# A gated mix of linear attention and an MLP on one core: first tiles reordered, two loads and two pieces of work moved up, denominators stored beside their product

## The chip, the cores and the metric

The kernel runs on one core of a Trainium2 chip. The metric is the device time of one execution in microseconds (us), lower is better. The kernel before takes 1105.97 us (median of 3 runs, 1105.97 to 1106.19).

The engines are called as the profile does: PE (matrix products), PEld (its weight loads), DVE (vector), ACT (activations), POOL (a second, slower vector engine) and SP (here it only starts DMAs). Each engine runs its instructions in program order and waits for others by semaphores. DMAs are started from SP's queue, a few from ACT's.

## The reference

```python
def _A_ref(x, wqkv, wo):
    qkv = (x @ wqkv).reshape(B, S, 3, H, Dh).transpose(2, 0, 3, 1, 4)
    q, k, v = qkv[0], qkv[1], qkv[2]
    phi = lambda t: jnp.where(t > 0, t + 1, jnp.exp(t)) + 1e-6
    pq, pk = phi(q), phi(k)
    kv = jnp.einsum("bhsd,bhse->bhde", pk, v)
    z = jnp.einsum("bhsd->bhd", pk)
    num = jnp.einsum("bhqd,bhde->bhqe", pq, kv)
    den = jnp.einsum("bhqd,bhd->bhq", pq, z)[..., None] + 1e-6
    return (num / den).transpose(0, 2, 1, 3).reshape(B, S, D) @ wo

def _B_ref(x, w1, b1, w2, b2):
    y = _layernorm(x, axis=-1)
    h = gelu_tanh(y @ w1 + b1)
    return h @ w2 + b2

g = sigmoid((x * gate_w).sum(-1, keepdims=True))
return g * a + (1 - g) * b        # a from _A_ref, b from _B_ref
```

S = 2048 rows, D = 576 columns, 32 heads of 18 columns, and an inner width F = 4608 of the MLP; everything is float32.

## The kernel before

All products run at float32 accuracy on operands that are split into a high part (rounded by ACT's copy) and a low part (the rest, by a DVE subtraction). So almost every operand costs one ACT and one DVE instruction ahead of PE, and both must be done before PE can use it. All 576 rows of a contraction are five blocks of 128, the last one holding 64 rows twice ("tail": `xe`, `we`, loaded by `load_twice`, L137), so that its high and low parts share a block. The profile gives L113 as the line of nearly every instruction, because they all pass through the class `InOrder` (L113), which keeps each engine in the order of the program text. So instructions are told apart by tiles.

**First tiles** (L481 to L577). After WARM passes of a product of ones, three x tiles of 128 rows are loaded together with the key and query weights, in four halves (KEY 0, KEY 1, QUERY 0, QUERY 1). The tile `t` holds a raw x tile, `s` raw weights, `y` the splits of both. The gate's weights (`gw`, landing in a corner of `accs`) are loaded by two DMAs on ACT's queue, turned by five small transposes and put beside the second half of the key weights.

**Sweep** (the loop behind `for n in range(FIRST, NT)`). One x tile after another: keys (project, then phi on ACT and DVE into `k`, then the split `ks`), the sums over keys times x, and queries into `accs` or `acc_right`. Preparations for later run beside it: a table `jobs` holds for each third of a tile what is issued there (`at(n, ...)`: n is three times the tile's position plus 0, 1 or 2). Among them are the first two chunks of w1 (`sum_w1`, `early_part`, stored by `store_early` to `w1d` through the stages `ys`), the normalised x pairs (`normal_pair`, `sum_pair`, `split_pair`, stored to `yd`), and the load of the value weights `wv` (`load_wv` at place 38). Every such load and store goes to SP's one queue, between the x tiles that are loaded two positions ahead.

**Attention loop** (`for i in range(NT)`). For each tile: POOL multiplies the queries with the sum of keys (`weigh`, tile `qz`, three buffers, four tiles ahead), DVE reduces the product to 32 denominators (`normalize`: reduction, addition, reciprocal) and normalises the queries, PE transposes them, ACT and DVE split the transposes (`qt`), and PE multiplies with `wp`. Sums for later pairs run on POOL beside it in `w_raw` and `accs`.

**MLP** (windows w = 0 to 17, and a tail). The first product is done with seven products of sums of blocks in place of eight (Strassen and Winograd), over 18 chunks of w1, first for one half of the rows and then for the other; the second product runs a window later (tiles `h`, `w_ops`). Sums of blocks of h (`sum_h`) and of w2 run on POOL or DVE by a written table of places (`do`, `do_first`: window, step 0 to 14, job). In window 10 the first half is finished: `add_combined` adds the MLP's part to the attention's part (tile `w_raw` or `pks`) and `store_out` sends it off, one tile a step.

Of the kernel before, what the change touches and what calls it, by code (L numbers as in the profile page):

```python
# [9 lines left out]
F32 = mybir.dt.float32  # L10
# [7 lines left out]
P = 128  # L18
# [18 lines left out]
EARLY = 2  # L37
EPS_PHI = 1e-6
EPS_LN = 1e-5
WARM = 6  # L40
FIRST = 3
LATE = 3
X_RING = 4
# [53 lines left out]
def heads(ap):  # L97
    return ap.rearrange("p (h d) -> p h d", d=DH)
# [18 lines left out]
def tile_gated_mix(ctx: ExitStack, tc: tile.TileContext, x, xm, xe, wm, we, wvm, wve, wo, um, ue, w2, b1, b2, gw, out):  # L117
# [17 lines left out]
        return ps[:, next(ff_banks)]  # L135

    def load_twice(dst, src, by=sp):  # L137
        for half in range(2):
            by.dma_start(dst[half * 64:(half + 1) * 64], src)

    def four_times(ap, half):

# [75 lines left out]
    def load_w(part, half, pieces=((0, 5),), by=sp):  # L218
        if (part, half) not in wraw:
            wraw[part, half] = wsp.tile([P, 5, HALF + 2], F32, name="s", tag="s")  # L220
        s = wraw[part, half]
        main = wm[part * 2 + half].rearrange("p (t n) -> p t n", t=4)
        tail = we[part * 2 + half]
        for t0, t1 in pieces:
            if t0 < 4:
                by.dma_start(s[:, t0:min(t1, 4), :HALF], main[:, t0:min(t1, 4)])
            if t1 == 5:
                load_twice(s[:, 4, :HALF], tail, by)
# [8 lines left out]
    def load_x(i):  # L237
        xraw[i] = yt.tile([P, 5, P], F32, name="t")
        sp.dma_start(xraw[i][:, 0:4], xm[i].rearrange("p (t n) -> p t n", t=4))
        load_twice(xraw[i][:, 4], xe[i])  # L240

    def split_x(i, pieces=((0, 5),)):
        if i not in xs:
            xs[i] = x_places[PLACE[i] % X_RING]
        to, src = xs[i], xraw[i]
        for t0, t1 in pieces:
            act.activation(to[:, t0:t1], src[:, t0:t1], AF.Copy)
            if t0 < 4:
                dve.tensor_sub(to[:, 5:9], src[:, 0:4], raw(to[:, 0:4]))
            if t1 == 5:  # L250
                dve.tensor_sub(to[64:P, 4], src[64:P, 4], raw(to[64:P, 4]))
# [16 lines left out]
    def project(i, part, half, order=BY_ROWS, n=None):  # L268
        w = W[part, half]
        p = banks[i, part, half] = ps[:, next(halves_in) if n is None else n]  # L270
        for m, (a, b) in enumerate(order):
            pe.matmul(p[:, :w.shape[2]], xs[i][:, a, :], w[:, b], start=(m == 0), stop=(m == len(order) - 1))
# [208 lines left out]
    first = ORDER[:FIRST]  # L481
    gwr = spare[0:1, :5 * P]
    load_x(first[0])
    load_w(KEY, 0, ((0, 1), (1, 2), (2, 4)), act)
    act.dma_start(gwr[:, :D], gw.rearrange("(a n) -> a n", a=1))
    act.dma_start(gwr[:, D:], gw[4 * P:D].rearrange("(a n) -> a n", a=1))
    act.activation(tiny, ones[:, 0:1], AF.Exp)
    load_w(KEY, 0, ((4, 5),))
    load_x(first[1])
    load_w(KEY, 1)  # L490
    load_x(first[2])
    load_w(QUERY, 0)
    load_xn(first[0])
    load_w(QUERY, 1)
# [12 lines left out]
    def first_keys(n, half):  # L507
        project(first[n], KEY, half, HI_FIRST, 3 * half + n)

    def first_queries(n, half):  # L510
        project(first[n], QUERY, half, HI_FIRST)

    def both_phi(n):
        for half in range(2):
            keys_phi(first[n], half)


    column = ps[:, 7, :5]
    for t in range(5):
        pe.transpose(column[:, t:t + 1], gwr[:, t * P:(t + 1) * P], ident[0:1, 0:1])  # L520
    first_keys(0, 0)
    split_x(first[1])
    first_keys(1, 0)
    dve.tensor_copy(wraw[KEY, 1][:, :, HALF:HALF + 1], column[:, :, None])
    dve.memset(wraw[KEY, 1][:, :, HALF + 1:HALF + 2], 1.0)
    split_w(KEY, 1)
    split_x(first[2])
    load_x(ORDER[3])
    first_keys(0, 1)
    first_keys(1, 1)  # L530
    both_phi(0)
    split_w(QUERY, 0)
    first_keys(2, 0)
    first_keys(2, 1)
    both_phi(1)
    keys_split(first[0])
    first_queries(0, 0)
    first_queries(1, 0)
    both_phi(2)
    phi(acc[first[0]], first[0], QUERY, 0)  # L540
    split_xn(first[0])
    moments_of(first[0])
    load_xn(first[2])
    first_queries(2, 0)
    phi(acc[first[1]], first[1], QUERY, 0)
    for part in range(2):
        add_products(first[0], part)
    split_w(QUERY, 1)
    phi(acc[first[2]], first[2], QUERY, 0)
    first_queries(0, 1)  # L550
    first_queries(1, 1)
    keys_split(first[1])
# [30 lines left out]
    def at(n, f, *args):  # L583
        jobs[n].append(lambda: f(*args))
# [8 lines left out]

    at(3 * 5, sp.dma_start, b1s, b1)
    at(31, load_wo)
    at(38, load_wv)
    for n, f in ((24, gates_in), (25, gates_act), (26, gates_out)):
        at(n, f, 0)
    def prepare_scale(q, n):
# [2 lines left out]
        at(n + 2, share_moments, q)  # L602

    for k in range(EARLY):
        n0 = (10, 13)[k]
        for n in range(4):
            at(n0 + n // 2, sum_w1, k, n, dve)
            at(n0 + 1 + n, early_part, k, n)
            at(n0 + 2 + n, store_early, k, n)
# [76 lines left out]
    qz, qt, tails, abank = {}, {}, {}, {}  # L686

    def weigh(i):
        qz[i] = qzp.tile([P, D], F32, name="qz")
        pool.tensor_tensor(out=qz[i], in0=acc[i], in1=zb, op=OP.mult)  # L690

    dens = {}

    def normalize(i, parts=(0, 1)):
        if 0 in parts:
            dens[i] = small.tile([P, H], F32, name="den")
        den = dens[i]
        if 0 in parts:
            dve.tensor_reduce(out=den, in_=heads(qz[i]), op=OP.add, axis=AX.X)
            dve.tensor_tensor(out=den, in0=den, in1=den0, op=OP.add)  # L700
            dve.reciprocal(den, den)
        if 1 in parts:
            dve.scalar_tensor_tensor(heads(acc[i]), heads(acc[i]), EPS_PHI, den[:, :, None].to_broadcast([P, H, DH]),
                                     op0=OP.add, op1=OP.mult)
# [102 lines left out]
        sp.dma_start(late_acc[i], acc[i])  # L807


    def w1_places(k, first):  # L810
        a, b = FIRST_W if first else LAST_W
        return wa if first else wb, wr(k)[:, a:b + 1]

    def split_w1(k, first):
        w, src = w1_places(k, first)
        act.activation(w[:, :, 0:3], src, AF.Copy)

    def split_w1_rest(k, first):
        w, src = w1_places(k, first)
        dve.tensor_sub(w[:, :, 3:5], src[:, :, 0:2], raw(w[:, :, 0:2]))  # L820
        dve.tensor_sub(w[64:P, :, 2], src[64:P, :, 2], raw(w[64:P, :, 2]))

# [253 lines left out]
    for p in range(WINDOWS - 1):  # L1076
        w = p + 1
        if p == 0:
            for x, m in zip((12, 13, 14, 15), (T3, T1, T2, T4)):
                do(0, x, sum_w2, 0, m, dve)  # L1080
        for m in range(7):
            x = 2 * m - 2 * (p == m == 0)
            do_first(w, x + -2.0, prepare_hi, p, m)
            do_first(w, x + -1.5, prepare_h_lo, p, m)
            do_first(w, x + -1.5, prepare_w2_lo, p, m)
        for x, *a in ((0, S3), (3.3, S2), (6, S1, dve), (7, S4)) if p < HALF_PAIRS else ((0, S3), (3, S2), (6, S1), (7, S4)):
            do(w, x, sum_h, p, *a)
        for x, m in ((4, S3), (8, S2), (9, S1), (11, S4)):
            do(w, x, give_back, p, m)
        if p + 1 < HALF_PAIRS:  # L1090
            for x, m in ((1, B11), (1, B21), (3, B12), (4, B22)):
                do(w, x, load_w2, p + 1, (m,))
        else:
            do(w, 5, load_w2, p + 1)
        if p + 1 < WINDOWS - 1:
            for x, *a in ((8, T3, dve), (9, T1), (10, T2, dve), (12, T4)) if p + 1 < HALF_PAIRS else ((9, T3), (10, T1), (11, T2), (12, T4)):
                do(w, x, sum_w2, p + 1, *a)

    for k in range(HALF_TIME):
        w, x = k // 2, 7 * (k % 2)  # L1100
        if k >= EARLY:
            x1 = x + (0, 0)[k % 2] if k + 1 < HALF_TIME else x - 1
            do_first(w, x1 + 0.5, split_w1, k, False)
            do(w, x1, split_w1_rest, k, False)
            if k + 1 < HALF_TIME:
                do(w, x1, load_w1, k + 1, False)
            do(w, x1, store_w1, k, True)
            do(w, x1 + 1, store_w1, k, False)
        if EARLY <= k + 1 < HALF_TIME:
            for x1, n in zip((-1, 0, 1, 2) if k < EARLY else ((0, 1, 2, 3), (0, 1, 2, 4))[k % 2], (0, 1, 3, 2)):  # L1110
                do(w, x + x1, sum_w1, k + 1, n, dve)
            x1 = x + (4 if k < EARLY else (4, 4)[k % 2])
            do_first(w, x1 + 0.5, split_w1, k + 1, True)
            do(w, x1, split_w1_rest, k + 1, True)
            if k + 2 < HALF_TIME:
                do(w, x1, load_w1, k + 2, True)

# [3 lines left out]
    for s in range(TPS):  # L1121
        if s < 6:
            do(p + 1, 6 + s, load_late, s, s)
        else:
            do(p + 2, 4, load_late, s, s - 6)
        do(p + 2, 1 + s, add_combined, p, s, s % 6)
        do(p + 2, 1 + s, store_out, s, s % 6)

    h_stage = h_ops.rearrange("p c k a n -> p (c k a n)")
    h_stages = [stage_of(h_stage[:, n * 10 * P:(n + 1) * 10 * P]) for n in range(3)]  # L1130
# [122 lines left out]
```

## Time and profile before

| what | value |
|---|---|
| median of the runs | 1105.97 us |
| profiled execution | 1106.91 us, its span 1105.2 us |
| DVE busy | 881.5 us |
| ACT busy | 571.1 us |
| POOL busy | 308.1 us |
| moved by DMA | 206.21 MB |
| start-up and first tiles | 0 to 40 us of the span |
| sweep over the other tiles | 40 to 186 us |
| moments, attention loop | 186 to 282 us |
| MLP windows from the second on | 306.8 us to the end |

A row of a timeline reads: start, duration, engine, line, operation, out<-in, shape, count, and in brackets how long the engine had been idle before it, and which engine's or transfer's end released it. Rows of windows give, for each engine, the busy time with the number of instructions in brackets; then the granted clock of PE, the DMA share and the rate.

### The profile page before, as it was taken

The numbers are of one execution on the slowest core, as the hardware profiler recorded it, in microseconds if no ns is written. First come the engines' busy times: TensorE is split into PE (matmuls) and PEld (weight loads), VectorE is DVE, ScalarE is ACT, GpSimd is POOL, SyncE is SP. The second block draws the span as 40 slices with busy tenths as digits, with TensorE's granted clock in tenths as the row PEclk, the third lists the DMA queues.
The fourth block names the chain that finished last, engine by engine and source line by source line (L and its number), as shares of the span: only waits on it lengthen the run. The fifth ranks groups of instructions, "written<-read, shape, count | busy, mean of one in ns | idle before, by whom it ended". The sixth has DMA issues, their size and how long they took to land.

```text
span 1105.2 us, 17967 instructions
## 1 busy us (share of the span) xinstructions
PE 1088.0 (98%) x6651; PEld 995.6 (90%) x6651; DVE 881.5 (80%) x1292; ACT 571.1 (52%) x917; POOL 308.1 (28%) x218
## 2 busy tenths in 40 slices
PE   8999998999999999999999999999999999999998
PEld 8989997999879989889898899989999999999998
DVE  4699987799788999999999996895666656656687
ACT  5667665344566555555556454355444444444450
POOL 0000000871022232222312223342543424334400
PEclk9999999999999999999999999999999999999999
DMA  6475766676964645536445498655544434434342
GB/s 176 139 260 185 244 212 233 217 293 235 341 206 156 201 165 197 187 138 241 165 163 192 144 342 353 204 155 198 150 112 134 141 106 145 144 108 142 105 153 86
DMA packets 126972, 206.21 MB, mean 187 GB/s; under 512 B 9743, under 2 KB 82735, under 8 KB 122918
## 3 DMA queue, kind: packets, MB, share of 16 engines
q1 hardware_dynamic: 126322, 204.49, 55.4%
q8 instruction: 52, 0.85, 0.3%
q10 hardware_dynamic: 564, 0.59, 0.2%
q14 instruction: 34, 0.28, 0.1%
HBM read 135.95 MB, written 69.09 MB: 186 GB/s over the span
## 4 chain that ended last, share of the span: by engine, by line
PE 80%; DVE 12%; DMA 3%; issue 2%; ACT 2%; SPq 1%; ACTq 0%; DVEq 0%
PE ps L113 80%; DVE h L113 2%; DVE accs L113 2%; DVE wa L113 2%; DVE w_ops L113 1%; SPq L113 1%; ACT wa L113 1%; DVE u L113 1%; DMA t<-in_xe 1%; DVE w_raw L113 1%; DVE den L113 1%; DMA w1d<-ys 0%; DMA w2r<-in_w 0%; DVE w2r L113 0%; DVE acc_right L113 0%
## 5 line engine op out<-in xcount | busy, mean ns | idle before, releaser
L113 PEld LDWEIGHTS ps<-w_ops,h 128*128 128x128 f32 x2856 | 427.1, 188 | 42.6 <-DVE w_ops L113 4.4
L113 PE MATMUL ps<-w_ops,h 128*128 128x288 f32 x2856 | 452.7, 295 | 2.4 <-DVE w_ops L113 1.8
L113 PE MATMUL ps<-y,wa 128*128 128x512 f32 x1008 | 277.2, 393 | 1.6 <-DVE wa L113 1.2
L113 POOL TENSOR_TENSOR u<-u 128x512 f32<-128x512 f32 x118 | 179.5, 1547 | 282.3 <-DVE h L113 148.8
L113 DVE TENSOR_TENSOR accs<-ps,accs 128x576 f32<-128x576 f32 x210 | 158.2, 754 | 107.3 <-PE ps L113 100.3
L113 PE MATMUL ps<-y,wb 128*128 128x512 f32 x756 | 202.4, 393 | 0.0
L113 PEld LDWEIGHTS ps<-y,wa 128*128 128x128 f32 x1008 | 174.1, 188 | 22.4 <-DVE wa L113 1.7
L113 ACT ACTIVATE u<-u,b1s 128x512 f32<-128x512 f32 x110 | 79.7, 725 | 217.2 <-DVE u L113 217.2
L113 PE MATMUL ps<-y 128*128 128x288 f32 (+1 forms) x1088 | 155.2, 302 | 6.0 <-ACT y L113 4.4
L113 DVE TENSOR_TENSOR h<-u,h 128x1024 fp32r<-128x1024 f32 x119 | 157.7, 1325 | 3.5 <-ACT h L113 3.5
L113 PEld LDWEIGHTS ps<-y 128*128 128x128 f32 x1088 | 151.7, 193 | 9.2 <-ACT y L113 5.1
L113 PEld LDWEIGHTS ps<-y,wb 128*128 128x128 f32 x756 | 132.4, 188 | 18.5 <-DVE u L113 0.7
L113 ACT ACTIVATE h<-u 128x1024 fp32r<-128x1024 f32 x119 | 125.2, 1052 | 39.2 <-PE ps L113 36.8
L113 POOL TENSOR_TENSOR w2r<-w2r 128x576 f32<-128x576 f32 x48 | 71.8, 1495 | 257.7 <-DVE w2r L113 134.2
L113 ACT ACTIVATE u<-ps 128x512 f32<-128x512 f32 x110 | 65.1, 594 | 101.8 <-PE ps L113 101.6
L113 DVE TENSOR_TENSOR u<-ps,u 128x512 f32<-128x512 f32 x110 | 75.3, 684 | 36.4 <-PE ps L113 23.4
L113 DVE TENSOR_TENSOR w_ops<-w2r,w_ops 128x576 fp32r<-128x576 f32 x119 | 97.9, 823 | 0.0
L113 ACT ACTIVATE w_ops<-w2r 128x576 fp32r<-128x576 f32 x119 | 79.6, 669 | 0.0
L113 PE MATMUL ps<-wp,qt 128*128 128x288 f32 x448 | 63.0, 297 | 0.0
L113 DVE TENSOR_TENSOR accs<-accs 128x384 f32<-128x384 f32 (+3 forms) x67 | 58.4, 881 | 3.1 <-DMA accs<-moments 1.7
L113 PEld LDWEIGHTS ps<-wp,qt 128*128 128x128 f32 x448 | 59.8, 188 | 0.0
L113 DVE TENSOR_TENSOR w_raw<-w_raw 128x384 f32<-128x384 f32 x64 | 53.7, 840 | 1.3 <-DMA w_raw<-in_ue 0.8
(139 smaller groups left out, 840.0 us busy)
## 6 DMA issues: line engine op xcount, KB each, us to landing
wa<-w1d SPq DMA_DIRECT2D x80, 320.0 KB
w2r<-in_w SPq DMA_DIRECT2D x72, 288.0 KB
w1d<-wa SPq DMA_DIRECT2D x16, 1280.0 KB
wb<-w1d SPq DMA_DIRECT2D x60, 320.0 KB
y<-yd SPq DMA_DIRECT2D x14, 1280.0 KB
w1d<-wb SPq DMA_DIRECT2D x16, 960.0 KB
w_raw<-in_um SPq DMA_DIRECT2D x96, 128.0 KB
yd<-ys SPq DMA_DIRECT2D x15, 640.0 KB
```

What stands on the lines that cost most here:

```text
L113: return lambda *args, **kwargs: self.tc.keep_in_program_order(op(*args, **kwargs))
```

## The change

Six edits:

- Start-up: three more warm-up products; the tails of weights and x come in one DMA of 128 rows (read twice) and no longer in two of 64; the gate's weights move from ACT's queue to SP's, behind the second x tile; the third x tile is loaded before the second half of the key weights; the first keys, phis, splits and queries of the three tiles are put in another order, one query half in a bank of its own.
- `load_wv` moves from place 38 to 35.
- The early work on w1 moves from places 10 and 13 to 9 and 12.
- The denominators are kept in 32 extra columns of `qz`, no longer in a tile `den` of their own.
- In window 10 one sum of blocks of h goes to DVE, and `add_combined` and `store_out` take steps 1, 2, 4, 5, 7, 8, 9, 10 in place of 1 to 8.
- The first split of w1 for chunk 2 (the first one in the MLP windows) is issued in two halves, ACT and DVE in turn.

```diff
-WARM = 6
+WARM = 9
...
     def load_twice(dst, src, by=sp):
-        for half in range(2):
-            by.dma_start(dst[half * 64:(half + 1) * 64], src)
+        (ld, r), (st, n) = src.ap
+        by.dma_start(dst, bass.AP(tensor=src.tensor, offset=src.offset, ap=[[0, 2], [ld, r], [st, n]]))
...
     load_x(first[0])
-    load_w(KEY, 0, ((0, 1), (1, 2), (2, 4)), act)
-    act.dma_start(gwr[:, :D], gw.rearrange("(a n) -> a n", a=1))
-    act.dma_start(gwr[:, D:], gw[4 * P:D].rearrange("(a n) -> a n", a=1))
+    load_w(KEY, 0, ((0, 1), (1, 2), (2, 4), (4, 5)), act)
     act.activation(tiny, ones[:, 0:1], AF.Exp)
-    load_w(KEY, 0, ((4, 5),))
     load_x(first[1])
+    sp.dma_start(gwr[:, :D], gw.rearrange("(a n) -> a n", a=1))
+    sp.dma_start(gwr[:, D:], gw[4 * P:D].rearrange("(a n) -> a n", a=1))
+    load_x(first[2])
     load_w(KEY, 1)
-    load_x(first[2])
     load_w(QUERY, 0)
...
     column = ps[:, 7, :5]
+    first_keys(0, 0)
+    split_x(first[1])
     for t in range(5):
         pe.transpose(column[:, t:t + 1], gwr[:, t * P:(t + 1) * P], ident[0:1, 0:1])
-    first_keys(0, 0)
-    split_x(first[1])
     first_keys(1, 0)
+    split_x(first[2])
+    first_keys(2, 0)
     dve.tensor_copy(wraw[KEY, 1][:, :, HALF:HALF + 1], column[:, :, None])
     dve.memset(wraw[KEY, 1][:, :, HALF + 1:HALF + 2], 1.0)
     split_w(KEY, 1)
-    split_x(first[2])
     load_x(ORDER[3])
     first_keys(0, 1)
     first_keys(1, 1)
+    split_w(QUERY, 0)
     both_phi(0)
-    split_w(QUERY, 0)
-    first_keys(2, 0)
     first_keys(2, 1)
     both_phi(1)
     keys_split(first[0])
     first_queries(0, 0)
     first_queries(1, 0)
+    split_xn(first[0])
     both_phi(2)
+    first_queries(2, 0, 3)
     phi(acc[first[0]], first[0], QUERY, 0)
-    split_xn(first[0])
+    split_w(QUERY, 1)
     moments_of(first[0])
     load_xn(first[2])
-    first_queries(2, 0)
+    phi(acc[first[2]], first[2], QUERY, 0)
     phi(acc[first[1]], first[1], QUERY, 0)
     for part in range(2):
         add_products(first[0], part)
-    split_w(QUERY, 1)
-    phi(acc[first[2]], first[2], QUERY, 0)
...
-    at(38, load_wv)
+    at(35, load_wv)
...
-        n0 = (10, 13)[k]
+        n0 = (9, 12)[k]
...
     def weigh(i):
-        qz[i] = qzp.tile([P, D], F32, name="qz")
-        pool.tensor_tensor(out=qz[i], in0=acc[i], in1=zb, op=OP.mult)
-
-    dens = {}
+        qz[i] = qzp.tile([P, D + H], F32, name="qz")
+        pool.tensor_tensor(out=qz[i][:, :D], in0=acc[i], in1=zb, op=OP.mult)
 
     def normalize(i, parts=(0, 1)):
+        den = qz[i][:, D:]
         if 0 in parts:
-            dens[i] = small.tile([P, H], F32, name="den")
-        den = dens[i]
-        if 0 in parts:
-            dve.tensor_reduce(out=den, in_=heads(qz[i]), op=OP.add, axis=AX.X)
+            dve.tensor_reduce(out=den, in_=heads(qz[i][:, :D]), op=OP.add, axis=AX.X)
...
-        for x, *a in ((0, S3), (3.3, S2), (6, S1, dve), (7, S4)) if p < HALF_PAIRS else ((0, S3), (3, S2), (6, S1), (7, S4)):
+        for x, *a in ((0, S3), (3.3, S2), (6, S1, dve), (7, S4)) if p < HALF_PAIRS else ((0, S3), (3, S2), (6, S1, dve), (7, S4)) if p == HALF_PAIRS else ((0, S3), (3, S2), (6, S1), (7, S4)):
             do(w, x, sum_h, p, *a)
...
-            do_first(w, x1 + 0.5, split_w1, k + 1, True)
-            do(w, x1, split_w1_rest, k + 1, True)
+            for own in (slice(0, 2), slice(2, 4)) if k < EARLY else (ALL,):
+                do_first(w, x1 + 0.5, split_w1, k + 1, True, own)
+                do_first(w, x1 + 0.5, split_w1_rest, k + 1, True, own)
...
-        do(p + 2, 1 + s, add_combined, p, s, s % 6)
-        do(p + 2, 1 + s, store_out, s, s % 6)
+        do(p + 2, (1, 2, 4, 5, 7, 8, 9, 10)[s], add_combined, p, s, s % 6)
+        do(p + 2, (1, 2, 4, 5, 7, 8, 9, 10)[s], store_out, s, s % 6)
```

The tables of places decide the order on the engines. Three places, before and after.

SP's queue in the sweep, near the load of the value weights, before (`t` is an x tile, `xn` the same rows untransposed, `accs<-in_xm` and `accs<-moments` feed a pair, `yd<-ys` stores one):

```order
L113 DMA accs<-in_xm 128x2x256
L113 DMA accs<-in_xe 128x1x128 x2
L113 DMA accs<-moments_104 128x512
L113 DMA wv<-in_wvm 128x2304
L113 DMA wv<-in_wve 64x576 x2
L113 DMA yd_128<-ys_551 128x2x640
L113 DMA t<-in_xm 128x512
L113 DMA t<-in_xe 64x128 x2
L113 DMA xn<-in_x 128x576
```

The same queue in the changed kernel:

```order
L113 DMA yd_131<-ys_547 128x2x640
L113 DMA wv<-in_wvm 128x2304
L113 DMA wv<-in_wve 128x1x576
L113 DMA yd_131<-y 128x640
L113 DMA t<-in_xm 128x512
L113 DMA t<-in_xe 128x1x128
L113 DMA xn<-in_x 128x576
L113 DMA accs<-in_xm 128x2x256
L113 DMA accs<-in_xe 128x1x128 x2
```

The value weights stood just ahead of the last x tile and behind the last pair's raw rows of the sweep; now they stand one x tile earlier, ahead of that tile and of those raw rows.

DVE's queue in the sweep, between the queries of the first tile of the loop and the next tile's keys, as a piece of the difference (`accs<-accs` are sums of w1 blocks, `ys` their split, `mt` scales of a pair):

```order
 L113 TENSOR_TENSOR xs<-xn,xs 128x64
+L113 TENSOR_TENSOR accs<-accs 128x384 x2
 L113 TENSOR_SCALAR mt<-sumsq 128x2
 L113 SCALAR_TENSOR_TENSOR accs<-ps,e 128x288 x2
+L113 TENSOR_TENSOR ys_545<-accs,ys_545 128x2x256
+L113 TENSOR_TENSOR ys_545<-accs,ys_545 64x2x128
 L113 TENSOR_TENSOR accs<-accs 128x384 x2
```

The first two sums of w1 now stand ahead of the queries' phi (`accs<-ps,e`), and the first split right behind it, where the first sums stood before.

DVE's queue at the beginning of window 10, piece of the difference (`h` and `w_ops` are split operands of the second product, `w_raw<-accs,omg,w_raw` is `add_combined`, `u<-u` a sum of blocks of h):

```order
 L113 SCALAR_TENSOR_TENSOR w_raw<-accs,omg,w_raw 128x576
 L113 TENSOR_TENSOR u<-ps,u 128x512
-L113 TENSOR_TENSOR accs<-ps,b2b 128x576
-L113 TENSOR_TENSOR h<-u,h 128x2x512
-L113 TENSOR_TENSOR w_ops<-w2r,w_ops 128x576
+L113 TENSOR_TENSOR h<-u,h 128x2x512
+L113 TENSOR_TENSOR w_ops<-w2r,w_ops 128x576
+L113 TENSOR_TENSOR u<-u 128x512 x2
```

The sum of blocks of h, two instructions that POOL had before, stands on DVE behind the operands of the second product.

More of the change, by code (lines that the diff above doesn't have):

```diff
@@ L508, in first_keys, with first_queries @@
         project(first[n], KEY, half, HI_FIRST, 3 * half + n)
-    def first_queries(n, half):
-        project(first[n], QUERY, half, HI_FIRST)
+    def first_queries(n, half, bank=None):
+        project(first[n], QUERY, half, HI_FIRST, bank)
     def both_phi(n):
@@ L807, in attend_out, with w1_places, split_w1, split_w1_rest @@
         sp.dma_start(late_acc[i], acc[i])
-    def w1_places(k, first):
+    def w1_places(k, first, own):
         a, b = FIRST_W if first else LAST_W
-        return wa if first else wb, wr(k)[:, a:b + 1]
-    def split_w1(k, first):
-        w, src = w1_places(k, first)
+        return (wa if first else wb)[:, own], wr(k)[:, a:b + 1][:, own]
+    ALL = slice(None)
+    def split_w1(k, first, own=ALL):
+        w, src = w1_places(k, first, own)
         act.activation(w[:, :, 0:3], src, AF.Copy)
-    def split_w1_rest(k, first):
-        w, src = w1_places(k, first)
+    def split_w1_rest(k, first, own=ALL):
+        w, src = w1_places(k, first, own)
         dve.tensor_sub(w[:, :, 3:5], src[:, :, 0:2], raw(w[:, :, 0:2]))
```

## The prediction

> **What bounds the kernel now.** I read the page's busy times first, then the list of what TensorE (PE) waited for, then the timeline of each engine around every wait in that list.
>
> ```profile
> PE 1088.0 (98%) x6651; PEld 995.6 (90%) x6651; DVE 881.5 (80%) x1292; ACT 571.1 (52%) x917; POOL 308.1 (28%) x218
> ```
>
> PE is busy for 1088.0 of 1105.2 us. No other engine comes near, so an edit can gain only where PE stands still, or where its clock is low. The list of PE's waits has all such places:
>
> ```profile
> PE ps L113 <- ACT y L113: 4.4, 3, 3.6
> PE ps L113 <- DVE w_ops L113: 1.8, 2, 1.5
> ...
> PE ps L113 <- DVE wa L113: 1.2, 1, 1.2
> PE ps L113 <- DVE k L113: 1.2, 2, 0.6
> ...
> PE ps L113 <- DVE acc_right L113: 0.7, 2, 0.5
> PE ps L113 <- DVE accs L113: 0.4, 2, 0.2
> ```
>
> Columns: total us, times, longest. Beside waits in the start-up, these few are all, about 9.7 us. Ends of PE's work are modelled, so the true loss is a little more than the idle shown, as the rows quoted for window 10 show: two matmuls start at 735.48, the third is due 0.13 us x 2 later at 735.75 and comes at 737.40, 1.65 late where the row says 1.50. I add 0.15 for each stall.
>
> **The change part by part.** Gains in us, counted on the profiled run.
>
> *a, start-up* (more warm-up, tails in one DMA, gate weights off ACT's queue, other order of the first tiles).
>
> ```profile
> 1.12 2.93 PE L113 MATMUL ps<-ones 128*128 128x128 f32 x12 [1.12 <-DVE ones L113]
> 5.63 0.71 PE L113 MATMUL ps<-accs 1*128 1x1 f32 x5 [1.58 <-DMA accs<-in_gw]
> 6.96 0.94 PE L113 MATMUL ps<-y 128*128 128x288 f32 x2 [0.63 <-ACT y L113]
> 8.07 8.12 PE L113 MATMUL ps<-y 128*128 128x288 f32 x40 [0.17 <-ACT y L113]
> ```
> ```profile
> 2.21 2.31 ACTq L113 DMA_DIRECT2D accs<-in_gw  x2
> 4.56 1.28 ACT L113 ACT_TABLE_LOAD   x1 [4.56 <-DMA t<-in_xm]
> 5.96 0.61 ACT L113 ACTIVATE y<-t 128x512 fp32r<-128x512 f32 x1
> ```
> ```profile
> 13.00:14.00 1.00, 1.00 (x6) 1.00 (x6) 0.66 (x1) 1.00 (x3) 0.00 (x0) 1.00 1.01 344
> 14.00:15.00 1.00, 1.00 (x10) 1.00 (x9) 1.00 (x2) 0.68 (x2) 0.00 (x0) 1.00 0.99 280
> ```
>
> ACT issues the two gate-weight DMAs until 2.21 + 2.31 = 4.52, loads its table until 5.84 and splits the first x tile at 5.96. With those DMAs on SP, one tail DMA (I take 0.6) stands there: the table load starts near 2.8 and the split near 4.4, or as soon as x is there. So the first matmuls come some 1.5 earlier (5.5), and the unbroken run, which also needs the other key pieces, about 1.1 earlier (7.0). Three more warm-up matmuls are six more passes of 2.93/12 = 0.244: the warm-up ends at 1.12 + 18 x 0.244 = 5.5, just when operands come, so it costs nothing unless operands come sooner. What an earlier start is worth depends on the clock. The two windows (first bracketed count: PE instructions) show 6 matmuls in a us up to 14.0 and 10 after it: PE runs at half speed until about 13.7, with the granted-clock column (third from the end) blind to it. At half speed a 288-column matmul takes 0.24, later 0.133. If the release stays at 13.7, the 1.1 earlier start gives 1.1/0.24 = 4.5 matmuls more by then, less 0.71/0.24 = 3 for the gate transposes, which filled a pause before and now stand among the matmuls; 1.5 x 0.133: gain 0.2. A release comes in steps: the half-speed stretch quoted in b spans about 3.4 us. One step earlier, near 10.3, PE does 3.4/0.133 - 3.4/0.24 = 11.4 matmuls more, 1.5 us: gain 1.7. One step later: -1.3. The stretch 6.88 to 10.29 before was busy for 3.16 of 3.41 us and released nothing; after, it is fuller. I take **1.0**, between 0.2 and 1.7, as I cannot tell them apart; ends -1.3 and 2.5 (released by 6.9, PE as fast as operands come; an estimate between 1.7 and a second step's 3.2).
>
> The Trainium skill ("TensorE: Matmul & The Clock Gate", Part 1) says that the clock is released after one busy window of about 3.4 us on a free-running counter, and asks a benchmark for at least 4 us of warm-up. The trace agrees with the step, but 8.07 to 13.7 was needed for one full window. By that rule the 4.4 us of warm-up would do it by 6.9: that is rival 3.
>
> *b, value weights moved three jobs up.*
>
> ```profile
> 160.43 1.96 SPq L113 DMA_DIRECT2D wv<-in_wve  x2
> 164.22 1.11 SPq L113 DMA_DIRECT2D t<-in_xe  x2
> ```
> ```profile
> 172.87 0.74 ACT L113 ACTIVATE y<-t 128x640 fp32r<-128x640 f32 x1 [7.47 <-DMA t<-in_xe]
> ```
> ```profile
> 173.66 5.54 PE L113 MATMUL ps<-y 128*128 128x288 f32 x28 [3.57 <-ACT y L113]
> ```
> ```profile
> 165.18 1.95 DVE L113 TENSOR_TENSOR accs<-accs 128x768 f32<-128x768 f32 x2 [1.65 <-DMA accs<-moments]
> ```
> ```profile
> 174.00:176.00 2.00, 2.00 (x11) 2.00 (x10) 1.85 (x5) 2.00 (x7) 0.00 (x0) 0.53 0.75 297
> ```
>
> The last x tile is issued behind 1.5 MB of wv, so it lands at 172.8, 8.6 after its issue; ACT stands for 7.47, PE for 3.57. The pause drops the clock (0.53, the third column from the end): 28 matmuls take 5.54, against 3.97 in the row of c. Together 3.57 + 0.15 + 1.57 = 5.3. Moved up, wv is issued near 143, with about 15 us of thin traffic behind it, and the tile can land near 166. Queued behind wv are then a store, the x tile before the last, and that pair's raw rows, which nobody waits for there: ACT takes that tile only 15 us before the one at 172.87. What is late next is DVE: it gets back the 1.65 that it waited for the moments, but the rest of its pair work stays ahead of its keys. I leave a stall of 1.0, enough to keep the clock: **4.3**; ends 3.6 (a stall of 1.7) and 5.2.
>
> *c, first w1 operands a third of a tile up.*
>
> ```profile
> 68.98 3.97 PE L113 MATMUL ps<-y 128*128 128x288 f32 x28 [0.58 <-DVE k L113]
> ```
> ```profile
> 48.82 0.46 DVE L113 SCALAR_TENSOR_TENSOR accs<-ps,e 128x288 f32<-128x288 f32 x1 [0.50 <-ACT e L113]
> 50.67 0.46 DVE L113 SCALAR_TENSOR_TENSOR accs<-ps,e 128x288 f32<-128x288 f32 x1 [1.39 <-ACT e L113]
> ```
>
> DVE is late for PE four times between 68 and 88 (k and accs: 1.2 + 0.4, with 0.15 each 2.2) and idles for 0.50 and 1.39 just before its chain of w1 work starts at 51. The early start uses that idle, 1.9 against a lateness of at most 0.62 at one place. No work is added. I leave 0.2: **2.0**; ends 1.0 (half the stalls recur ahead) and 2.2.
>
> *d, denominators in the product's tile.* POOL's next multiply into that tile then waits for the normalising DVE instruction that reads the denominators, and no longer for the reduction only.
>
> ```profile
> 210.19 0.92 DVE L113 SCALAR_TENSOR_TENSOR accs<-accs,den 128x576 f32<-128x576 f32 x1
> 219.80 1.49 DVE L113 SCALAR_TENSOR_TENSOR accs<-accs,den 128x576 f32<-128x576 f32 x1
> ```
> ```profile
> 216.88 1.84 POOL L113 TENSOR_TENSOR w_raw<-w_raw,kvs 128x768 f32<-128x768 f32 x1
> 219.23 1.44 POOL L113 TENSOR_TENSOR qz<-accs,pks 128x576 f32<-128x576 f32 x1 [0.50 <-DVE den L113]
> ```
> ```profile
> 222.65 0.60 PE L113 MATMUL ps<-accs 128*128 128x128 f32 x4
> 226.92 0.60 PE L113 MATMUL ps<-accs 128*128 128x128 f32 x4
> ```
>
> The normalising takes 1.49 when it starts beside qz, ending 0.62 after POOL, and 0.92 where it hardly overlaps: it is held. After, it runs ahead of qz and is 0.57 shorter. But in five iterations POOL has w_raw work behind qz, and now that stands in front of DVE's next addition to den: qz 1.44, w_raw 1.84, 0.57 for addition and reciprocal (from 219.23, when the reduction was done, to 219.80) and 0.92 make 4.8 from one normalising to the next, over PE's 226.92 - 222.65 = 4.27. Five times 0.5 is 2.5, against a lead of 222.65 - 221.29 = 1.4 plus those 0.57. So some 0.5 appears in the middle, about as much again where other DVE work stands beside qz, and the 0.7 + 0.3 at 257 and 262 goes: **0**; ends -2.0 and 1.0. The Trainium skill ("SBUF — State Buffer", "SBUF: two separate sides") has VectorE instructions with two SBUF inputs and GpSimd's take one port pair by exclusive lock for a whole instruction; the 1.49 agrees, and the rule speaks against this edit.
>
> *e, a sum to DVE and combines spread out, window 10.*
>
> ```profile
> 735.48 0.42 PE L113 MATMUL ps<-w_ops,h 128*128 128x288 f32 x2
> 737.40 0.80 PE L113 MATMUL ps<-w_ops,h 128*128 128x288 f32 x4 [1.50 <-DVE w_ops L113]
> ```
> ```profile
> 728.05 10.44 POOL L113 TENSOR_TENSOR u<-u 128x512 f32<-128x512 f32 x6 [7.26 <-DVE h L113]
> 733.30 2.30 DVE L113 TENSOR_TENSOR h<-u,h 128x1024 fp32r<-128x1024 f32 x1
> ```
>
> Six POOL sums in a row hold DVE's h split (2.30) and, behind it, w_ops. After, four stand there and a combine leaves the place ahead; the two sums that DVE gets come after w_ops. Of 1.65 I leave 0.25: **1.4**; ends 0.5 and 1.6.
>
> *f, the first w1 split in two halves.*
>
> ```profile
> 306.78 0.73 PE L113 MATMUL ps<-y,wa 128*128 128x512 f32 x2 [0.24 <-ACT wa L113]
> ```
> ```profile
> 306.75 1.95 DVE L113 TENSOR_TENSOR wa<-w_raw,wa 128x1024 fp32r<-128x1024 f32 x2 [2.17 <-ACT wa L113]
> ```
>
> PE waits 0.24 for ACT's half and 1.25 for DVE's. In halves DVE's first part takes about 1.0 and starts 0.6 sooner. Of 0.24 + 1.25 + 0.3 I leave 0.3: **1.5**; ends 1.0 and 1.8.
>
> **Sum.** 1.0 + 4.3 + 2.0 + 0 + 1.4 + 1.5 = 10.2: the profiled run, 1106.91 (1.7 around its span), goes to 1096.7; it stood 0.94 above the median, so the median goes from 1105.97 to **1095.8**.
>
> **Rivals.** *2, DVE stays the limit:* its work is only moved, so stalls come back one place on. b 3.6, c 1.0, d -2.0, the rest as above: 6.5, 1099.5. For it: DVE is packed from 51 to 92 and the lock in d; against: the idle named in b and c is real. *3, the clock comes up by 6.9:* a gives 2.5, bounded by operands, 1094.3. Against it: the busy 6.88 to 10.29 that released nothing. *4, the wv move does nothing,* as its bytes meet stores and tiles near 143 and the stall moves to an earlier tile: b 0, 1100.1. Against: ACT has spare time there. *5, slower:* the lock in the attention loop. If in the five w_raw iterations the normalising is held by a second w_raw instruction as well, one turn is 4.8 + 1.84 = 6.6 against 4.27; five cost 11.7, and the sum is -1.5, 1107.5. It decides from 10.2/5 = 2.0 an iteration; I reckon 0.5.
>
> **Chances.** Forecast 0.52, rival 2 0.21, rival 3 0.12, rival 4 0.09, rival 5 0.03, something unnamed 0.03. All lows together give 2.8 and all highs 14.3; 8 in 10 lie from 1092.0 to 1100.5, which takes in rivals 2, 3 and 4. A measurement here tells 0.2%, 2.2 us, from no change: faster 0.91, same 0.05, slower 0.04.
>
> **What would show it.** a: ten matmuls a us from 10.3 (1.8), 13.7 (0.4) or 17.1. b: no PE idle at 170, the clock at 1.00 there, the x tile split before 168. c: no stall at 69 to 88, and DVE's gap at 49 to 51 filled. d: the normalising at 0.9, den's addition long in 216 to 239, a PE wait for acc_right in the middle of the loop. e, f: the waits for w_ops and wa under 0.3. Wrong would make it: PE waits of over 1 us at new places, or DVE idle behind a DMA in the sweep.

## The result and the profile after

| | time, us | against the kernel before (95% interval) |
|---|---|---|
| before | 1105.97 (1105.47 to 1106.19, 4 runs) | |
| changed | 1112.45 (1111.98 to 1113.68, 4 runs) | 1.0061 (1.0044 to 1.0078) |

The change makes the kernel 6.5 us slower, where I had forecast 10 us faster. The time lies outside the range and beyond every rival.

The page's busy line and the list of PE's waits, of the changed kernel (span 1110.7 us):

```profile
PE 1091.2 (98%) x6657; PEld 997.7 (90%) x6657; DVE 883.5 (80%) x1296; ACT 571.5 (51%) x918; POOL 303.1 (27%) x216
```
```profile
PE ps L113 <- ACT y L113: 6.1, 4, 3.4
PE ps L113 <- DVE k L113: 3.4, 1, 3.4
PE ps L113 <- DVE qt L113: 2.0, 1, 2.0
PE ps L113 <- DVE ones L113: 1.1, 1, 1.1
PE ps L113 <- ACT accs L113: 0.9, 1, 0.9
PE ps L113 <- DVE accs L113: 0.6, 3, 0.2
PE ps L113 <- DVE wa L113: 0.3, 1, 0.3
PE ps L113 <- DVE acc_right L113: 0.2, 1, 0.2
```

What I meant to remove is gone or smaller: no wait for w_ops (1.8 before), wa 0.3 (1.2), acc_right 0.2 (0.7). But there are four waits for y in place of three, one of 3.4 for k, one of 2.0 for qt and one for accs.

The order of PE's work is the same in both kernels from the first sums (`xs,ks`) on. So the start of the same matmul in both traces can be compared; the difference is PE's lag, and where the lag grows or shrinks is where time was lost or won. This ledger, worked out from the starts, is used below for all runs (e1 to e13 are the experiments; us; negative: ahead of the kernel before). The stretches are given in the times of the kernel before. Each column is one profiled run, and row a differs between runs by more than most terms: e5 and e7 start with the same instructions and stand at -1.57 and +0.91.

| stretch | what lies in it | forecast | changed | e1 | e3 | e5 | e13 |
|---|---|---|---|---|---|---|---|
| 0 to 62 | a, start-up and first tiles | -1.0 | +6.68 | +0.58 | +0.36 | -1.57 | -1.70 |
| 62 to 100 | c, w1 operands | -2.0 | -1.44 | -1.44 | -1.42 | -1.45 | -1.43 |
| 100 to 190 | b, value weights | -4.3 | +0.80 | -4.05 | -3.99 | -5.12 | -4.35 |
| 190 to 262 | d, denominators | 0 | +1.50 | +2.94 | +3.03 | -0.02 | +0.01 |
| 303 to 330 | f, w1 split in halves | -1.5 | -0.18 | -0.26 | +0.18 | -0.29 | -0.25 |
| 700 to 745 | e, window 10 | -1.4 | -1.71 | -1.71 | -1.72 | -1.72 | -1.70 |
| whole | | -10.2 | +5.45 | -4.04 | -3.77 | -10.24 | -9.14 |

Two terms are off by far: a by 7.7 and b by 5.1. Both trace to one thing, the merged tail. In the start-up, ACT's queue, ACT, PE, and the windows of the changed kernel:

```profile
2.22 1.12 ACTq L113 DMA_DIRECT2D s<-in_we  x1
```
```profile
12.92 0.44 ACT L113 ACTIVATE y<-s 128x288 fp32r<-128x288 f32 x1 [4.75 <-DMA s<-in_we]
```
```profile
13.41 2.06 PE L113 MATMUL ps<-y 128*128 128x288 f32 x6 [3.38 <-ACT y L113]
```
```profile
7.00:10.00 3.00, 1.78 (x6) 1.46 (x6) 1.05 (x2) 0.88 (x2) 0.00 (x0) 1.00 0.16 55
```

The tail of the first key weights, one DMA now, is issued at 2.22 and is there only at 12.9: 10.7 us for 147 KB. ACT stands for 4.75 and PE for 3.38. From 7 to 10 us the DMA share (last but one) is 0.16, that is 2.6 of 16 DMA engines, at 55 GB/s. In the kernel before the shares of these three us are 0.57, 0.72 and 1.06. The completion marks of the two forms in the trace say why: a tail in two DMAs ends in 16 marks each (5.68 to 6.20 us for the first one), the merged one in two that come with data (12.75 and 12.90) and one right after the issue (3.58). It looks as if two of the sixteen engines carry it. The 10.7 us are not this DMA's alone: two merged x tails, issued at 1.26 and 2.46, end in two marks each as well (the last at 7.26 and 13.09), and from 7 to 10 us the trace has 78 packets of the weights' rows (1152 bytes) beside 72 of the x tails' (512 bytes).

In the sweep, SP's queue, ACT and DVE of the changed kernel around the last two x tiles, and PE:

```profile
150.49 4.76 SPq L113 DMA_DIRECT2D yd<-y  x1
155.29 0.83 SPq L113 DMA_DIRECT2D t<-in_xm  x1
156.17 0.67 SPq L113 DMA_DIRECT2D t<-in_xe  x1
156.94 5.49 SPq L113 DMA_DIRECT2D xn<-in_x  x1
```
```profile
167.78 0.74 ACT L113 ACTIVATE y<-t 128x640 fp32r<-128x640 f32 x1 [4.61 <-DMA t<-in_xe]
177.75 0.74 ACT L113 ACTIVATE y<-t 128x640 fp32r<-128x640 f32 x1 [5.13 <-DMA t<-in_xe]
```
```profile
168.54 1.01 DVE L113 TENSOR_TENSOR y<-t,y 128x512 fp32r<-128x512 f32 x2 [4.89 <-ACT y L113]
179.13 0.46 DVE L113 SCALAR_TENSOR_TENSOR k<-ps,e 128x288 f32<-128x288 f32 x1
```
```profile
179.73 5.51 PE L113 MATMUL ps<-y 128*128 128x288 f32 x28 [3.42 <-DVE k L113]
```

Behind `wv<-in_wve`, also a merged tail, the issue of a small store holds SP's queue for 4.76 and that of an `xn` load for 5.49. In the first 200 us such long issues (over 1.4 us, on SP) are frequent only where tails are merged: 11 here and 12 in e2, against none in the kernel before and two and three in e1 and e3. What an issue waits for in that time, no run shows. The tile before the last is issued at 156 and its tail is late at 167.8, that of the last one at 177.8. DVE, held 4.89 at 168.5 by the first, comes late with k (179.59); the last tile's high part is split no earlier than 178.49 either. PE loses 3.42 and runs at half clock once more (0.50 from 182 to 184). So the stall that b was to remove is back at the same tile, the last one of the sweep.

### The profile page after: what moved, and what is told of

It reads as the page before. It is cut to its first block, busy times and chain, and to the rows that moved or that the text cites. A ratio compares the mean times of both kernels' runs of the same rounds, so it can differ in the third digit from the quotient of the medians.

```text
span 1110.7 us, 17958 instructions
## 1 busy us (share of the span) xinstructions
PE 1091.2 (98%) x6657; PEld 997.7 (90%) x6657; DVE 883.5 (80%) x1296; ACT 571.5 (51%) x918; POOL 303.1 (27%) x216
## 4 chain that ended last, share of the span: by engine, by line
PE 76%; DVE 12%; DMA 5%; ACT 3%; issue 2%; SPq 1%; ACTq 0%; DVEq 0%
PE ps L113 76%; DVE h L113 2%; DVE accs L113 2%; DMA s<-in_we 2%; DVE wa L113 2%; DVE w_ops L113 1%; DVE qz L113 1%; SPq L113 1%; DMA t<-in_xe 1%; ACT wa L113 1%; DVE u L113 1%; ACT e L113 1%; DMA w_raw<-in_ue 1%; DVE w2r L113 1%; DVE w_raw L113 1%
## 5 line engine op out<-in xcount | busy, mean ns | idle before, releaser
L113 POOL TENSOR_TENSOR u<-u 128x512 f32<-128x512 f32 x116 | 176.0, 1542 | 280.7 <-DVE h L113 149.0
```

Of the source, the lines that this page charges most:

```text
L113: return lambda *args, **kwargs: self.tc.keep_in_program_order(op(*args, **kwargs))
```

## The experiments

Theory A: the DMA that reads its 64 rows twice is slow by itself and holds up the queue. Theory B: the new order of loads, or the place of wv, is at fault. Each experiment is compared with the kernel before on the same chip (its median there: 1107.14 for e1 to e4, 1107.16 for e5 to e8, 1106.96 for e9 to e12, 1106.90 for e13).

**e1, tails in two DMAs again** (the changed kernel, one edit undone):

```diff
-        (ld, r), (st, n) = src.ap
-        by.dma_start(dst, bass.AP(tensor=src.tensor, offset=src.offset, ap=[[0, 2], [ld, r], [st, n]]))
+        for half in range(2):
+            by.dma_start(dst[half * 64:(half + 1) * 64], src)
```

> The changed kernel with one edit undone: load_twice is again two DMAs of 64 rows. Theory A (the single DMA, which reads its 64 rows twice, is slow by itself and holds up what is issued behind it): the first sums over keys (PE's first xs,ks matmul, 27.26 us in the kernel before, 33.33 in the changed one) start at 26 to 27; the wait of 3.4 us for DVE k near 176 shrinks below 1.2; the time is 1098 to 1102. Theory B (the new order of the loads in the start-up and the place of wv cost the time, whatever the form of the tails): the first sums stay above 31, a wait of 3 us stays in the sweep, and the time is 1109 to 1113.

Measured 1104.83 (1103.21 to 1106.02), ratio 0.9976 (0.9966 to 0.9985). The first sums start 0.58 late (at 27.84, where I expected 26 to 27), and ACT waits for the last x tile for 1.70 in place of 5.13. A holds: the changed kernel's loss turns into a gain. The time is 3 us over what I expected; that is about d, 2.94 in the ledger, taken up below.

**e2, the merged tail alone on the kernel before** (the same edit the other way round).

> The kernel before with one edit of the change alone: tails in one DMA that reads its rows twice. Theory A: the tail of the first key weights lands over 8 us after its issue, the first sums start at 31 or later, x tiles of the sweep land late at one place or more, and the time is 1111 to 1120. Theory B: within 2 us of the kernel before, 1104 to 1108.

Measured 1118.41 (1118.08 to 1118.56), ratio 1.0102 (1.0087 to 1.0117): 11 us slower, with nothing else changed. ACT's rows:

```profile
10.52 0.44 ACT L113 ACTIVATE y<-s 128x288 fp32r<-128x288 f32 x1 [2.57 <-DMA s<-in_we]
```
```profile
183.19 0.74 ACT L113 ACTIVATE y<-t 128x640 fp32r<-128x640 f32 x1 [11.65 <-DMA t<-in_xe]
```

The lag is 6.13 after the first tiles and grows by 4.88 at the last x tile, behind the value weights. The form alone does it, as A expected in every point. The two ledgers also add up to the changed kernel's: in the start-up 6.13 for the form (e2) and 0.58 for the rest (e1) make 6.71, measured 6.68; from 100 to 190, 4.88 for the form and -4.05 for the moved value weights make 0.83, measured 0.80. So the move of the value weights gave its gain in the changed kernel too, and the form took it away.

**e3, one DMA of 128 rows without a repeated dimension.** The tail rows lie twice in memory, laid out so before the launch.

```diff
-        (ld, r), (st, n) = src.ap
-        by.dma_start(dst, bass.AP(tensor=src.tensor, offset=src.offset, ap=[[0, 2], [ld, r], [st, n]]))
+        by.dma_start(dst, src)
...
-        tail = w[512:].reshape(64, n, k).transpose(1, 0, 2)
+        tail = np.tile(w[512:].reshape(64, n, k).transpose(1, 0, 2), (1, 2, 1))
```

> The changed kernel, but the 64 tail rows lie twice in memory, so that one DMA of 128 rows loads a tail without a repeated outer dimension. Theory A as a matter of how the DMA is spread (an outer dimension of 2 leaves it to two DMA engines): as fast as with two halves, or up to 1 us faster as an issue is saved per tail, 1097 to 1102, and each of these DMAs ends in 16 parts. Theory C (one DMA for 128 short rows is slow in any form): as the changed kernel, 1110 to 1114.

Measured 1103.88 (1101.26 to 1105.74), ratio 0.9970 (0.9958 to 0.9982), 2 us over what was expected for the same reason as e1. These DMAs end in 16 marks each, and the tail of the first key weights, issued at 2.21, is there at 7.22. One DMA is not slow; the outer dimension of 2 is.

**e4, e1 with the denominators in their own tile.**

```diff
-        qz[i] = qzp.tile([P, D + H], F32, name="qz")
+        qz[i] = qzp.tile([P, D], F32, name="qz")
...
-        den = qz[i][:, D:]
...
+            dens[i] = small.tile([P, H], F32, name="den")
+        den = dens[i]
...
```

> As e1_two_halves, and the denominators again in a tile of their own. If the denominators' place costs what the two traces show between the loop's start and 270 us (the lag of PE grows from 5.8 to 7.5 us): 1.2 to 2.2 us faster than e1_two_halves, no wait for DVE qt of 2 us in the loop, and again two short waits for acc_right. If that growth was brought in from the sweep by late work: within 0.5 us of e1_two_halves.

Measured 1101.11 (1099.63 to 1102.80), ratio 0.9946 (0.9928 to 0.9965): 3.7 us faster than e1 between the medians, more than I expected. The ledger of 190 to 262 falls from 2.94 to 0.02, and the two waits for acc_right are back (0.7). So it is d, to about 2.9 of the 3.7.

**e12, the denominators in the product's tile alone, on the kernel before.**

> The kernel before, with the denominators in the product's tile alone. If this edit costs what the ledgers of e1 and e4 differ by: 1.5 to 3.2 us slower, with a wait for DVE qt of 1 to 2 us near 245 and the additions to den held for 1.5 us in the five iterations with w_raw. My own step put it at 0 with ends -2.0 and 1.0: within 1 us.

Measured 1108.80 (1107.52 to 1111.74), ratio 1.0020 (1.0009 to 1.0032), and a wait for qt of 2.0. So the edit costs 1 to 3.5 us by itself, by the interval. The profiled run lost 2.63, of which only 1.42 lies in the loop; 1.16 came from 100 to 190, around the last x tile (granted clock 0.50 from 174 to 178), where this edit changes nothing. The rows are those of the changed kernel, DVE, POOL and PE in the loop:

```profile
228.93 1.63 DVE L113 TENSOR_TENSOR qz<-qz,den 128x32 f32<-128x32 f32 x1
250.44 1.41 DVE L113 TENSOR_TENSOR mt<-mt 128x2 f32<-128x2 f32 x1
```
```profile
228.66 1.84 POOL L113 TENSOR_TENSOR w_raw<-w_raw,kvs 128x768 f32<-128x768 f32 x1
250.41 1.42 POOL L113 TENSOR_TENSOR qz<-acc_right,pks 128x576 f32<-128x576 f32 x1 [1.31 <-DVE mt L113]
```
```profile
254.22 2.91 PE L113 MATMUL ps<-wp,qt 128*128 128x288 f32 x20 [2.02 <-DVE qt L113]
```

The addition of 32 numbers a row takes 1.63, as it waits for the end of w_raw (228.66 + 1.84 = 230.50); an operation on two numbers a row (mt) takes 1.41 beside qz. The second kind I had not listed: qz now starts right behind the normalising, so it takes what comes next on DVE, whatever that is.

**e5, both mended** (e3 and e4 together).

> The changed kernel with both faults mended: tails whose rows lie twice in memory, and the denominators in a tile of their own. If these two are what the change lost, the other edits give what the ledger of PE's lag says (value weights 4.2, w1 operands 1.3 to 1.8, window 10 1.7): 1099 to 1102, 5 to 8 below the kernel before of the same chip, and neither the 2 us wait for DVE qt nor one over 1.5 in the sweep is left. If one of the two costs something else: within 1 us of e4_halves_own_den or e3_rows_twice.

Measured 1098.83 (1096.66 to 1100.52), ratio 0.9925 (0.9909 to 0.9940): 8 us faster than the kernel before, a little better than expected. The profiled run reached a lag of -10.24. That this is my sum of 10.2 is luck: it was the fastest of five runs (1096.66), d's edit is undone in it, a and b gave more than forecast and f almost nothing.

**e6, e5 with the value weights back at place 38.**

> As e5, with the load of the value weights back at place 38. If the move is worth what I forecast (4.3; the ledger of e1_two_halves has 4.2): 3.5 to 5 us slower than e5, with the last x tile of the sweep late by some 3 us for PE and half clock after it. If single issues of the tails already freed the queue, so that the place does not matter: within 1 us of e5.

Measured 1100.95 (1099.75 to 1101.78), ratio 0.9943 (0.9930 to 0.9956): 2.1 us slower than e5 (ledger of 100 to 190: -2.53 in place of -5.12). Less than the 3.5 to 5 expected: with half as many issues for tails, the last tile comes earlier even from the old place (e11, the kernel before with such tails, has -2.49 in this stretch without the move).

**e7, e5 with the first w1 split in one piece.**

```diff
-            for own in (slice(0, 2), slice(2, 4)) if k < EARLY else (ALL,):
+            for own in (ALL,):
```

> As e5, with the first split of w1 in the MLP windows in one piece. My step (the gain of the halves stands): 1.5 us slower than e5. Rival (DVE is late 10 us later in the same window anyway, and takes most of it back): at most 0.6 us slower; waits for ACT wa and DVE wa of 1.5 together come back, and the wait for ACT accs of 0.8 after them goes.

Measured 1100.46 (1097.98 to 1102.78), ratio 0.9937 (0.9919 to 0.9955). The 1.6 between the medians would speak for my step, but the ledger doesn't: from 303 to 330 it is +0.02 here and -0.29 in e5, while the profiled start-ups differ by 2.5. The waits moved as the rival says: wa 1.2 + 0.2 is back, accs 0.8 is gone. The halves gain 0.3. PE, ACT and DVE of the changed kernel show where the rest goes:

```profile
314.84 0.74 PE L113 MATMUL ps<-y,wa 128*128 128x512 f32 x2 [0.34 <-DVE wa L113]
326.43 1.06 PE L113 MATMUL ps<-w_ops,h 128*128 128x288 f32 x6 [0.85 <-ACT accs L113]
```
```profile
325.12 0.72 ACT L113 ACTIVATE u<-u,b1s 128x512 f32<-128x512 f32 x1 [2.81 <-DVE u L113]
325.75 0.63 ACT L113 ACTIVATE accs<-ps 128x576 f32<-128x576 f32 x1
```
```profile
322.35 1.55 DVE L113 TENSOR_TENSOR wb<-w_raw,wb 128x768 fp32r<-128x768 f32 x2
323.92 0.56 DVE L113 TENSOR_TENSOR w_raw<-w_raw 128x384 f32<-128x384 f32 x1
324.40 0.69 DVE L113 TENSOR_TENSOR u<-ps,u 128x512 f32<-128x512 f32 x1
```

PE comes 1.4 earlier and finds DVE where it always was: u only behind the split of wb and a sum, ACT behind u, and the result bank that PE needs next behind ACT.

**e8, e5 with the start-up of the kernel before** (its order, six warm-up products; tails in one DMA each).

> As e5, with the start-up of the kernel before (six warm-up products, gate weights on ACT's queue, old order of the first tiles), but tails in one DMA each. My step (the new start-up gives 0.2 to 1.7): 0.2 to 1.7 us slower than e5. Rival (the gate transposes among the first matmuls keep the clock down a step longer): equal or faster by up to 1.5 us.

Measured 1098.85 (1098.57 to 1099.52), ratio 0.9926 (0.9913 to 0.9938): the same median as e5, but within 1 us, where e5 spreads over 4. That is the time the rival gave, and not mine; e13 speaks against the rival's cause. So the new start-up wins nothing on the median, and the question is what spreads it.

**e9 and e10, the gate transposes behind the third tile's keys; e10 with 14 warm-up products too.** Theory G: the transposes among the first matmuls keep the clock down. Theory P: the pause after the warm-up drops it.

> As e5_rows_own_den, with the five small gate transposes moved behind the first keys of the third tile. Theory G (these transposes do not count as work for the clock, so the stretch that they break keeps half speed: e3, e6 and e7 ran at half clock from about 9 to 15, e5 did not): the half-clock stretch ends one step, 3.4 us, earlier in such runs; median 1097 to 1098.3. Theory P (the pause of PE between the warm-up's end near 5.2 and the run from 7.1 drops the clock, the transposes are innocent): as e5, 1098 to 1100, and spread as wide.

> As e9, with 14 warm-up products instead of 9, which fill PE until about 7.1. Theory P: the clock, once up, does not drop any more, at most the first 7 us are at half speed, and the runs come together at the level of the profiled run of e5: 1095.5 to 1097.5, spread under 2 us. Theory G: no better than e9, and 0 to 0.4 slower as the first two key matmuls start later.

Measured 1101.77 (1100.16 to 1102.72) and 1100.53 (1100.30 to 1100.71), ratios 0.9954 (0.9941 to 0.9966) and 0.9945 (0.9933 to 0.9958). Both are slower than e5, against both theories: the split of the second key half now waits for the late transposes, PE stands for 1.7 at 13, and a stretch at 0.50 follows (16 to 19 us in e9, 17 to 20 in e10). They settle nothing between G and P, but e10's five runs lie within 0.4.

**e13, e5 with 14 warm-up products, the transposes left in place.**

```diff
-WARM = 9
+WARM = 14
```

> As e5_rows_own_den with 14 warm-up products and the gate transposes where the change put them. Theory P (the pause between the warm-up and the first matmuls drops the clock again): the clock stays up from the warm-up on, the runs come together within 1.5 us, at the level of the fastest runs of e5, 1096 to 1097.5. Theory G (the transposes among the first matmuls do it): as e5, 1097 to 1100 and spread over 3 us or more.

Measured 1097.81 (1097.53 to 1097.98), ratio 0.9917 (0.9904 to 0.9931): five runs within 0.45 us, and the best median of all, 9.1 us below the kernel before (its interval overlaps with e5's, so the gain over e5 is in the spread). P holds against G, at a level 0.3 above what I expected. The edit shortens the pause and lengthens the warm-up (6.12 for 4.21) at once; which of the two keeps the clock up, no run separates. Windows of e6, a run that lost the clock, and of e13:

```profile
7.00:9.00 2.00, 1.49 (x9) 1.28 (x10) 1.51 (x3) 2.00 (x4) 0.00 (x0) 1.00 0.62 162
9.00:11.00 2.00, 2.00 (x12) 1.71 (x11) 1.67 (x6) 0.14 (x1) 0.00 (x0) 0.52 1.08 325
11.00:13.00 2.00, 2.00 (x10) 2.00 (x9) 0.01 (x1) 1.41 (x1) 0.00 (x0) 0.50 0.94 272
```
```profile
7.00:9.00 2.00, 1.44 (x12) 1.21 (x10) 0.97 (x2) 1.68 (x4) 0.00 (x0) 1.00 0.47 131
9.00:11.00 2.00, 2.00 (x16) 1.62 (x16) 1.91 (x5) 0.59 (x1) 0.00 (x0) 1.00 1.01 327
11.00:13.00 2.00, 2.00 (x18) 2.00 (x17) 0.31 (x3) 1.05 (x1) 0.00 (x0) 1.00 0.89 239
```

In e6 PE pauses for 1.51 before 7.51 and is at 0.5 from about 9 to 15; in e13 the warm-up lasts until 7.2, the pause is 0.56, and the clock stays at 1.00.

**e11, the kernel before with rows twice alone.**

> The kernel before, with the tail rows twice in memory and one DMA of 128 rows each. If fewer issues on SP's queue are worth something by themselves (in e6 the old place of wv cost 2.6 us less than in the kernel before): 2 to 4 us faster, most of it at 170 us. If not: within 1 us of the kernel before.

Measured 1105.44 (1104.04 to 1106.98), ratio 0.9987 (0.9978 to 0.9997): 1.4 us faster, less than the 2 to 4 expected. The lag is -2.73 at 190, and 1.6 of it is lost again near 309: PE waits for wa as before, and this time its matmuls come at half pace after it (granted clock 0.59, 0.50 and 0.61 in the stretches from 306 to 310).

## Why the prediction was wrong

- **a.** The step that failed: "With those DMAs on SP, one tail DMA (I take 0.6) stands there". I priced its issue (it took 1.12) and not its landing; the new `load_twice` had no term of its own anywhere. The landing cost 6.7 in the start-up in place of a gain of 1.0, and e2 has 6.1 from it alone. ACT stood for 4.75 until the tail was there. The Trainium skill says it ("DMA: Bandwidth & Descriptors", Why a DMA increments its semaphore by 16 and not by 1): the number of engines that carry a DMA is the largest up to 16 that divides the slowest dimension of both sides; its Rules for kernel authors name a leading repeat of c copies as confining it to at most c. The two marks and the share of 0.16 agree. The prediction had not used this rule. With the tails mended the times of a are as worked out: in e3 the table load starts at 2.73 (forecast 2.8), the first matmuls at 5.34 (5.5), the unbroken run at 7.25 (7.0). The worth is not: with the same start-up e3, e5, e6 and e7 stand at +0.36, -1.57, +0.71 and +0.91 in the ledger. It hangs on the clock as I said, but not as a step earlier or later: from 9 us on e5 does 10 matmuls a us until 13, at a clock of 1.00; e3, e6 and e7 do 5 to 8 a us until 15, at 0.50, though e6 and e7 did 8 in the us before. So the clock is up after the warm-up and drops again in some runs, after the pause. The granted-clock column does not tell all: in e4 it reads 1.00 while PE does 6 or 7 a us from 9 to 16.
- **b.** "the tile can land near 166" holds where tails are not merged (ACT splits it at 166.2 in e1), and the term is 4.05 there, against 4.3. In the changed kernel the stretch gave +0.8, by the same DMA form: wv's own tail, the x tails and the long issues behind them. Rival 4 has the outcome, a stall that is not removed, by another cause.
- **c.** Right in kind, 1.44 for 2.0. One more wait came ahead of the four, worth 0.4.
- **d.** The mechanism, the additions held behind w_raw, is there as worked out: one turn takes 4.5 (normalising at 230.98 and 235.50), I had 4.8. The size was off: a loss of 1.4 to 3.0 in the loop, not 0, and the wait came for qt, not for acc_right. I had left out in detail what qz now hits behind the normalising, the splits of wb and the work on mt. Where the 2 us wait comes at a bad moment, the clock drops as well; that is most of the difference between 1.5 and 2.9.
- **e.** Right: 1.71 for 1.4.
- **f.** Right at its place, 1.4 of 1.5, and wrong in the sum, 0.2: "Of 0.24 + 1.25 + 0.3 I leave 0.3" does not ask who is late next. DVE was, 12 us later. That is what rival 2 says, at a place where I had not put it.
- **The range.** It was made of the terms that I saw. It ended at 1100.5 and the slowest rival at 1107.5, since an edit that looked like a saved issue had no end on the bad side. Both signs named for being wrong came: PE waits of over 1 us at new places (3.42 for k, 2.02 for qt), and DVE idle behind a DMA in the sweep (4.89).

## What to carry to other kernels

A DMA that is written in another form is another DMA: before fewer issues are counted as a gain, ask how many engines carry it (how many completion marks, what DMA share while it runs alone) and what waits behind it in its queue. When a stall is removed, follow the engine that it waited for to its next delivery: PE arrives there earlier by what was won. A buffer that is freed later by an edit lets the next instruction start at a worse time for its neighbours, also where nobody waits for the buffer.

## What the runs showed of the hardware

- A DMA of 128 rows of 1152 bytes took 10.7 us with a repeated outer dimension of 2, with two x tails of the same form beside it. Two DMAs of 64 rows took 3.7 and 2.1 in the kernel before (2.49 to 6.20 and 4.48 to 6.62), and one of 128 rows without the repeat took 5.0 in e3 (2.21 to 7.22).
- The clock of PE can drop after pauses much shorter than the half-clock stretch that follows: in e1 a wait of 2.01 us is followed by 0.50 from 244 to 246, in the changed kernel a wait of 2.02 is not (1.00 from 254 to 258). In the start-up a pause of 1.18 is followed by 0.50 in e3, one of 1.16 is not in e9. In e6 a pause of 1.51 us is followed by some 6 us at half clock. The Trainium skill ("TensorE: Matmul & The Clock Gate", Part 1) has the window in which PE's work is counted run free of the program, which agrees with the difference between like pauses. That a whole idle window is needed for the drop, as its table has it, is not what these runs show: the pauses here were of 1.2 to 2.0 us.
- An addition of 128x32 numbers on DVE takes 0.19 alone and up to 1.63 beside a POOL instruction, an operation on 128x2 0.16 alone and up to 1.41: in both rows shown it ends within 0.1 us of the POOL instruction, so the wait does not follow the size of DVE's work.
